# One matmul on 112 columns for two on 64 and 48 in the state products, and the decay sums F of ten tiles in column quarters

## The chip, the cores and the metric

The kernel runs on one core of one Trainium2 chip. The metric is the device time of one execution in microseconds (us): the median of the executions shown, where one execution is the time of the whole program on that core. A profile is taken of one execution by the hardware profiler; it records every instruction of the five engines with its start and its duration. PE is TensorE's matmuls, PEld its weight loads, DVE is VectorE, ACT is ScalarE, POOL is GpSimd.

## The reference

A gated linear recurrence (batch 4, 8 heads, 768 steps, head dimension 48), and behind it a maxout layer. All is float32.

```python
def _attn_ref(q, k, v, a_re, a_im):
    mag = np.sqrt(a_re * a_re + a_im * a_im)
    scale = np.minimum(mag, 0.999) / (mag + 1e-06)
    a_re_n, a_im_n = (a_re * scale, a_im * scale)
    ...
    for t in range(S):
        ar, ai = (a_re_n[:, :, t, :, None], a_im_n[:, :, t, :, None])
        new_re = ar * S_re - ai * S_im
        new_im = ar * S_im + ai * S_re
        kv = np.einsum('bhd,bhe->bhde', k[:, :, t], v[:, :, t])
        S_re, S_im = (new_re + kv, new_im)
        y[:, :, t] = np.einsum('bhd,bhde->bhe', q[:, :, t], S_re)

def _moe_ref(x, w1, w2, w3, w_out):          # x: 3072 x 384
    h = np.maximum(np.maximum(x @ w1, x @ w2), x @ w3)   # 3072 x 768
    return h @ w_out                          # 3072 x 384
```

## The kernel before, in words

The recurrence is computed in blocks of 128 time steps. There are 24 tiles, one for each batch and block: `x = 2 * g + c`, with g from 0 to 11 and c called x or y in the schedule (`Fx:3` is step F of group 3, c = 0). Six values of g in a row (s = 0 to 5) walk through one pair of batches. A tile holds 8 heads of 48 columns and two chunks of 64 steps; the chunks lie on the two halves of the 128 rows (partitions) of the keys and values.

For each tile the steps on TensorE are, by their names in the schedule:

- `cs` sums the phases along time; `sums` sums the log magnitudes `Ln` within a chunk (64 rows, 64 columns, line 649).
- `F` forms the decay sums of a head for 29 cut positions: the weights are a head's 48 columns of `Ln`, the moving operand is the matrix `cuts` (lines 679 to 695). Two forms stand in the code. The plain one takes each chunk alone: 64 rows, 48 weight columns, 29 moving columns, 16 matmuls a tile. The quartered one takes both chunks at once: 128 rows, weights in pieces of 32 and 16 columns, 58 moving columns (`cuts` has zeros where a row belongs to the other chunk), again 16 matmuls a tile. ScalarE then takes the exponential of the sums (`f0` to `f3`).
- `tpk` and `tpq` transpose the rotated keys and queries, which are 112 columns wide (cosine part in columns 0 to 47, sine part in 64 to 111, zeros between); `A` and `B` are scores, `y` the outputs.
- `dk` (line 802) forms the state products: for each of 8 head and chunk pairs (4 pairs where s = 5) and each of two row halves j, the keys' 64 rows by 112 columns times the values' 64 rows by 48 columns. `h1` and `h3` add the result to the state `g`.

The maxout layer's matmuls are `U..` (tile `up`), `P1` to `P7`, `Px`, `Py` (tile `op`, a seven-product scheme) and, for the first group, `O`. The set-up has `T`, `M` and `pw` matmuls.

The order of all work on every engine is written out by hand: `SCHEDULE` is a list of words `step:group`, and each engine executes its instructions in that order. Three further lists say how a word is executed. `SLOTS` gives each matmul step its PSUM buffer, `OTHER` moves a step to another engine, and `QUARTERS` names the words whose matmuls are issued on column pieces of 32. In the kernel before, `QUARTERS` holds `cs`, `P`, `U` words but no `F` and no `dk`.

So TensorE executes matmuls of five shapes of array tile, by rows and columns: 128 by 128 (`U`, `P`, `O` in the plain form), 128 by 64 (`cs`), 128 by 32 (`A`, `B`, `y` and all quartered words), 64 by 64 (`sums`, `F`, `dk`) and 64 by 128 (`tpk`, `tpq`). Each float32 matmul call appears in the trace as two weight loads and two matmuls; a transpose appears as one of each.

The plain F loops are these lines:

```python
for ch in range(2) if not quarter else ():
    r = slice(ch * L64, (ch + 1) * L64)
    mm(out=ps[o:o + D, ch, n * NF:(n + 1) * NF], lhsT=T["Ln", g][r, h * D:(h + 1) * D],
       rhs=cuts[r, ch], start=True, stop=True)
for lo, hi in ((0, 32), (32, D)) if quarter else ():
    mm(out=T["Fp", x][o + lo:o + hi, :, n * NF:(n + 1) * NF],
       lhsT=T["Ln", g][:, h * D + lo:h * D + hi], rhs=cuts, start=True, stop=True)
```

Of the kernel before, what the change touches and what calls it, by code (L numbers as in the profile page):

```python
# [138 lines left out]
QUARTERS = set("""  # L139
csx:0 csx:1 csx:3 csx:4 Py:2 Px:2 csy:5 csx:5 csx:6 csy:6 csx:8 csx:9 csy:9 csx:10 P1:8 P5:8 P7:8 csy:10 P6:8 Px:8  # L140
Py:8 U12:9 P6:9 Py:9 P2:9 csx:11 csy:11 P4:9 U11:10 U01:10 Py:10 Px:10 U02:10 U12:10 P1:10 U11:11 P2:10 U12:11 P3:10
U01:11 U02:11 Py:11 P1:11 Px:11 P2:11 P5:11 P7:11 P6:11 P3:11 P4:11
""".split())

ROOMS = {0: "w1", 3: "w2", 6: "wo", 11: "w1", 1: "w2", 9: "H", 10: "S", 2: "H", 4: "S", 5: "H", 7: "S", 8: "H"}
# [4 lines left out]
def kernel(  # L150
# [16 lines left out]
    L64 = 64  # L167
    DD = L64 + D
# [28 lines left out]
    T = {}  # L197
# [29 lines left out]
    def banks(nm, n=None):  # L227

        ps = psum.tile([P, 2, 512], FP, tag="ps" + next(slots), name=nm)
        T["ps"] = ps  # L230
        return ps if n is None else ps.rearrange("p a n -> p (a n)")[:, 0:n]
# [149 lines left out]
    def heads(view):  # L381

        dims = [list(d) for d in view.ap]
        return bass.AP(view.tensor, view.offset, dims[:-1] + [[P - D, 2], [1, D]])
# [114 lines left out]
    def both(t, h):  # L499

        return t[:, h]
# [291 lines left out]
    def state(x, name):  # L793

        s = x // C % NS
        G = T["G", x] = gs[x % 4]

        def four(t):

            return heads(t).rearrange("p i j d -> p j i d")  # L800

        if name == "dk":
            ps = T["dk", x] = banks("dk")
            for n in range(H if s < NS - 1 else 4):
                ch, i = divmod(n, 4)
                for j in range(2):
                    r = slice(j * L64, (j + 1) * L64)
                    for lo, hi in ((0, L64), (L64, DD)):
                        mm(out=ps[lo:hi, j, n * D:(n + 1) * D], lhsT=both(T["Uk", x], n)[r, lo:hi],
                           rhs=T["v", x][r, ch, i, j * D:(j + 1) * D], start=True, stop=True)  # L810
        elif name[0] == "h" and name[1:].isdigit():
            c, i = divmod(int(name[1:]), 2)
            new = four(G[0:DD, 1] if c == 0 else gs[(x + C) % 4][0:DD, 0])
            dk = T["dk", x][0:DD, :, 0:DM].rearrange("p j (c i d) -> p c j i d", c=2, d=D) if i else None
            if c > 0 and s == NS - 1 or s + c + i == 0:
                return True
            if i == 0:
                F = T["F", x][0:DD, :, :, CD:CD + 1].rearrange("p (c i) j n -> p c j i n", c=2)
                dve.tensor_tensor(out=new, in0=four(G[0:DD, c]), in1=F[:, c].to_broadcast([DD, 2, 4, D]), op=OP.mult)
            elif s + c == 0:  # L820
                act.copy(out=new, in_=dk[:, c])
            else:
                dve.tensor_tensor(out=new, in0=new, in1=dk[:, c], op=OP.add)
        else:
            return False
        return True
# [158 lines left out]
    def run(name, g):  # L985
# [13 lines left out]
        elif name[0] in "TtMm" and name[1:].isdigit():  # L999
            product(name[0], int(name[1:]))  # L1000
        elif name[0] == "W":
            i = int(name[2:])
            weight_load(i) if name[1] == "L" else weight_step(i, name[1])
        elif name[0] in "Uu" and name[1:].isdigit():
            up(g, int(name[1]), int(name[2]), name[0])
        elif name[0] in "Uu" and name[1:3].isdigit():
            up_one(2 * g + "xy".index(name[3]), int(name[1]), int(name[2]), name[0])
        elif name in SEVEN or name in ("ox", "oy") and g > 0:
            seven(g, name)
        elif name[0] == "J":  # L1010
            join(name[1])
        elif name[-1] in "01" and gates(g, [int(name[-1])], name[:-1]):
            pass
        elif gates(g, list(range(C)), name):
            pass
        else:
            c = "xy".index(name[-1])
            x, name = g * C + c, name[:-1]
            if name in ("Lr", "Li"):
                load_a(g, c, *(("ar", a_re) if name == "Lr" else ("ai", a_im)))  # L1020
            elif name in ("Lk", "Lq"):
                load_kq(g, c, *(("k", k) if name == "Lk" else ("q", q)))
            elif name == "Lv":
                load_v(g, c)
            else:
                assert angles(g, c, name) or turns(g, c, name) or factors(x, name) or scores(x, name) \
                    or state(x, name) or outputs(x, name) or project(x, name), name
# [45 lines left out]
```

## Time and profile before

| | |
|---|---|
| time, median of 2 runs | 543.97 us (543.03 to 544.91) |
| profiled execution, its own time | 543.5 us |
| its span, first to last instruction | 541.8 us |
| mean granted TensorE clock | 0.99 |
| PE busy | 514.8 us (95%), 11146 matmuls |
| PEld busy | 433.8 us (80%) |
| DVE, ACT, POOL busy | 482.4, 362.0, 66.6 us |

The 1.7 us between span and time lie around the program. Almost all lines of the program run through one helper, so that the profile names line 210 for them; the groups are told apart by the tiles that an instruction writes and reads, written out<-in (`dk<-vb,uk`: the state products from values and keys), and by shape (`64*48 64x48`: 64 rows and 48 columns of weights; moving operand of 64 rows and 48 columns). A matmul's recorded duration is its latency; several of them are in flight at once, so the pace is read from starts, or from how long a known number of them takes.

### The profile page before, as it was taken

The page shows a single profiled execution, that of the slowest core. Times are in us where ns is not written, and L with a number is a line of the kernel's source. Part 1 is how long each engine was busy: PE and PEld are TensorE (multiplying, and loading weights), DVE is VectorE, ACT ScalarE, POOL GpSimd, SP SyncE. Part 2 cuts the span into 40 slices and gives each one's busy share as a digit, 9 for nine tenths or more (in the row PEclk, how much of TensorE's full clock was granted, in tenths as well). Part 3 has the DMA queues.
Part 4 walks back from the last instruction along what each step waited for, and adds up shares of the span by engine and source line. Part 5 has one row for each costly group of instructions (what it writes and reads, how often), then busy time and mean ns, then how long its engine had stood idle before and what let it go on. Part 6 is the DMA issues. An engine that isn't in the chain of part 4 may idle for free.

```text
span 541.8 us, 24758 instructions
## 1 busy us (share of the span) xinstructions
PE 514.8 (95%) x11146; PEld 433.8 (80%) x11146; DVE 482.4 (89%) x756; ACT 362.0 (67%) x634; POOL 66.6 (12%) x111
## 2 busy tenths in 40 slices
PE   3499899999999999999899999999999989999996
PEld 1366878788988989888788988888889877977865
DVE  5999999999999899999899989899999879998343
ACT  6999988786777876678697695685763865451100
POOL 8416300200300300100200020020200120000000
PEclk9969999999999999999999999999999999999999
DMA  8999775343154242727024344034153252000001
GB/s 211 287 257 206 174 135 99 65 83 76 32 106 78 57 76 48 137 40 149 4 54 78 69 79 99 4 69 82 26 114 59 37 94 53 19 18 5 4 2 59
DMA packets 140841, 45.27 MB, mean 84 GB/s; under 512 B 130368, under 2 KB 138560, under 8 KB 140736
## 3 DMA queue, kind: packets, MB, share of 16 engines
q1 hardware_dynamic: 136272, 37.76, 32.9%
q0 software_dynamic: 4464, 5.94, 6.4%
q8 instruction: 87, 1.43, 1.1%
q14 instruction: 18, 0.15, 0.1%
HBM read 33.02 MB, written 4.72 MB: 70 GB/s over the span
## 4 chain that ended last, share of the span: by engine, by line
PE 88%; ACT 5%; DVE 2%; issue 2%; POOL 2%; DMA 1%; DVEq 0%; POOLq 0%; ACTq 0%
PE up L210 34%; PE op L210 24%; PE y L210 7%; PE A L210 6%; PE tp L210 4%; PE dk L210 4%; PE sums L210 3%; PE cs L210 2%; PE wm L210 2%; PE F L210 2%; PE B L210 1%; DMA ar<-nf 1%; ACT L210 1%; ACT xhx L210 1%; ACT L L210 1%
## 5 line engine op out<-in xcount | busy, mean ns | idle before, releaser
L210 PE MATMUL up<-xhx,w 128*128 128x256 f32 (+1 forms) x1278 | 179.0, 381 | 1.6 <-issue 1.5
L210 PEld LDWEIGHTS up<-xhx,w 128*128 128x128 f32 (+1 forms) x1278 | 140.3, 149 | 31.0 <-issue 2.9
L210 ACT ACT_TABLE_LOAD x51 | 65.4, 1283 | 1.6 <-PEq L1057 0.8
L210 POOL DMA_DIRECT2D ar<-nf x40 | 32.8, 1246 | 165.0 <-DVE ar L210 131.1
L210 PE MATMUL op<-wo,xhx 128*32 128x192 f32 (+3 forms) x418 | 50.0, 366 | 0.0
L210 ACT COPY atm<-B 32x128 f32<-32x128 f32 x96 | 24.5, 255 | 33.5 <-DVE atm L210 18.2
L210 DVE TENSOR_TENSOR Q<-Q,f 112x512 f32<-112x512 f32 (+1 forms) x48 | 45.0, 951 | 1.0 <-ACT Q L210 1.0
L210 ACT ACTIVATE f<-F 48x232 f32<-48x232 f32 x96 | 34.3, 358 | 15.1 <-PE F L210 9.7
L210 PE MATMUL y<-QG,g 112*32 112x64 f32 x1408 | 38.5, 219 | 1.8 <-issue 1.8
L210 PE MATMUL y<-atm,vb 128*32 128x64 f32 x1152 | 39.2, 220 | 0.9 <-ACT uk L210 0.9
L210 PEld LDWEIGHTS op<-wo,xhx 128*32 128x32 f32 (+1 forms) x418 | 34.4, 139 | 5.6 <-issue 2.4
L210 PEld LDWEIGHTS y<-atm,vb 128*32 128x32 f32 x1152 | 34.1, 109 | 4.8 <-issue 3.7
L210 PEld LDWEIGHTS y<-QG,g 112*32 112x32 f32 x1408 | 35.3, 109 | 2.0 <-issue 1.9
L210 PE MATMUL A<-Q,K 112*32 112x80 f32 x1536 | 32.8, 238 | 0.9 <-ACT t L210 0.9
L210 DVE COPY_PREDICATED atm<-masko,A 128x256 f32<-128x256 uint8 x72 | 31.6, 439 | 1.4
L210 PE MATMUL op<-wo,strassen 128*128 128x192 f32 (+1 forms) x272 | 32.6, 327 | 0.0
L210 PEld LDWEIGHTS A<-Q,K 112*32 112x32 f32 x1536 | 28.9, 112 | 4.6 <-issue 2.0
L210 PE MATMUL op<-w,strassen 128*32 128x192 f32 (+1 forms) x296 | 32.5, 328 | 0.0
L210 PEld LDWEIGHTS op<-wo,strassen 128*128 128x128 f32 (+1 forms) x272 | 28.4, 152 | 2.3
L210 DVE TENSOR_TENSOR ot<-ot,op 128x384 f32<-128x384 f32 (+1 forms) x56 | 25.6, 464 | 4.2 <-PE op L210 3.5
L210 PEld LDWEIGHTS op<-w,strassen 128*32 128x32 f32 (+1 forms) x296 | 28.0, 147 | 1.6 <-issue 0.3
L210 DVE TENSOR_TENSOR xhx<-xhx,up 128x768 f32<-128x768 f32 x22 | 20.9, 949 | 9.0 <-PE up L210 8.9
(152 smaller groups left out, 1048.9 us busy)
## 6 DMA issues: line engine op xcount, KB each, us to landing
ai<-in_a_im_dram SPq DMA_DIRECT2D x24, 192.0 KB, 3.9
ar<-in_a_re_dram SPq DMA_DIRECT2D x24, 192.0 KB, 3.3
q<-in_q_dram SPq DMA_DIRECT2D x96, 48.0 KB, 2.7
k<-in_k_dram SPq DMA_DIRECT2D x96, 48.0 KB, 2.7
vb<-in_v_dram SPq DMA_DIRECT2D x96, 48.0 KB, 3.1
out_dram<-ot SPq DMA_DIRECT2D x23, 192.0 KB, 3.1
Ln<-e POOLq DMA_DIRECT2D x8, 384.0 KB, 5.7
w<-in_moe_w_dram SPq DMA_DIRECT2D x3, 767.2 KB, 7.3
```

The lines of the kernel that those rows point to most:

```text
L210: ins = f(*a, **kw)
```

## The change

All 24 `dk` words and ten `F` words (`Fx:2` to `Fx:11`) are added to `QUARTERS`. For `F` this chooses the quartered form that is in the code. For `dk` the loop over column pieces now asks the list too: a `dk` word in it issues one matmul on all 112 columns in place of one on columns 0 to 63 and one on columns 64 to 111. The schedule's order, the PSUM buffers and the engines stay.

```diff
 QUARTERS = set("""
 ...
-U01:11 U02:11 Py:11 P1:11 Px:11 P2:11 P5:11 P7:11 P6:11 P3:11 P4:11
+U01:11 U02:11 Py:11 P1:11 Px:11 P2:11 P5:11 P7:11 P6:11 P3:11 P4:11 dkx:0 dky:0 dkx:1 dky:1 dkx:2 dky:2 dkx:3 dky:3
+dkx:4 dky:4 dkx:5 dky:5 dkx:6 dky:6 dkx:7 dky:7 dkx:8 dky:8 dkx:9 dky:9 dkx:10 dky:10 dkx:11 dky:11 Fx:2 Fx:3 Fx:4
+Fx:5 Fx:6 Fx:7 Fx:8 Fx:9 Fx:10 Fx:11
 """.split())
...
                 for j in range(2):
                     r = slice(j * L64, (j + 1) * L64)
-                    for lo, hi in ((0, L64), (L64, DD)):
+                    for lo, hi in ((0, DD),) if T["word"] in QUARTERS else ((0, L64), (L64, DD)):
                         mm(out=ps[lo:hi, j, n * D:(n + 1) * D], lhsT=both(T["Uk", x], n)[r, lo:hi],
                            rhs=T["v", x][r, ch, i, j * D:(j + 1) * D], start=True, stop=True)
```

## The prediction

> **What bounds the kernel now.** I read the page's totals and its chain first, then TensorE's share by stretch and its waits, and only then the instructions that change.
>
> ```profile
> span 541.8 us, 24758 instructions
> PE 514.8 (95%) x11146; PEld 433.8 (80%) x11146; DVE 482.4 (89%) x756; ACT 362.0 (67%) x634; POOL 66.6 (12%) x111
> ...
> PE 88%; ACT 5%; DVE 2%; issue 2%; POOL 2%; DMA 1%; DVEq 0%; POOLq 0%; ACTq 0%
> ```
>
> ```profile
> core 0: us, PE busy (x) PEld busy (x) DVE busy (x) ACT busy (x) POOL busy (x), PEclk, DMA share, GB/s
> 0.00:72.00 72.00, 52.87 (x902) 38.09 (x902) 63.75 (x104) 65.40 (x118) 31.75 (x69) 0.93 0.93 224
> 72.00:500.00 428.00, 424.47 (x9445) 367.72 (x9444) 402.83 (x626) 294.75 (x511) 34.88 (x42) 1.00 0.35 66
> ```
>
> ```profile
> PE y L210 <- issue: 1.8, 1, 1.8
> PE up L210 <- issue: 1.5, 1, 1.5
> ```
>
> The first fence gives TensorE 88% of the chain that ended last. The second, busy time by stretch, shows where: before 72 us it works 53 of 72 us, from 72 to 500 us all but 3.5 of 428 us, at the full granted clock. The third, TensorE's waits after 72 us, names those 3.5 us: two pauses in which it waited for nothing that the profile shows. So behind 72 us no other engine delays TensorE, and what its stream gains or loses there moves the end one for one. Only two of the 24 `dk` steps lie ahead, and only the second, at 57 us, has cover, for the chain runs over VectorE there:
>
> ```profile
> 38.86 1.12 PE dk L210 x53
> ...
> 57.65 0.95 DVE ai L210
> 58.60 0.87 DVE w L210
> ```
>
> **What the two steps cost today.** The trace does not give an instruction's pace by its duration, since several are in flight. I take it from starts, comparing a single with a double burst that were entered alike, so that entry and exit cancel.
>
> ```profile
> 102.31 1.09 PE L210 MATMUL dk<-vb,uk 64*64 64x48 f32 x64
> 103.33 0.27 PE L210 MATMUL tp<-ident,uq 64*112 64x64 f32 x2
> ...
> 291.92 2.02 PE L210 MATMUL dk<-vb,uk 64*64 64x48 f32 x128
> 293.87 0.43 PE L210 MATMUL op<-w,strassen 128*128 128x192 f32 x1
> ...
> 141.03 0.56 PE L210 MATMUL F<-cuts,Ln 64*48 64x29 f32 x32
> 141.51 0.26 PE L210 MATMUL y<-atm,vb 128*32 128x64 f32 x4
> ...
> 270.67 0.92 PE L210 MATMUL F<-cuts,Ln 64*48 64x29 f32 x64
> 271.52 0.48 PE L210 MATMUL up<-xhx,w 128*128 128x256 f32 x1
> ...
> 169.35 0.46 PE L210 MATMUL B<-QB,KB 112*32 112x32 f32 x32
> 169.62 0.39 PE L210 MATMUL cs<-w,upto 128*32 128x192 f32 x4
> ```
>
> `dk`: 128 matmuls take 1.95 us (291.92 to 293.87), 64 take 1.02 us. The 64 more cost 0.93 us. They go in turn to four array tiles (two row halves by columns 0-63 and 64-111), 16 to each, so a tile with 64 weight columns takes 58 ns a matmul. `F`: 32 more cost 0.85 - 0.48 = 0.37 us, 8 on each of four tiles: 46 ns. `B`: 32 in 0.27 us, 8 on each of four column tiles: 34 ns.
>
> What sets these paces? Not the moving operand: F moves 29 columns and takes 46 ns, B moves 32 and takes 34. By weight columns they stand in order: 32 gives 34 ns, 48 gives 46, 64 gives 58, which is 12 ns for each 16 columns. The weight loads say the same:
>
> ```profile
> L210 PEld LDWEIGHTS up<-xhx,w 128*128 128x128 f32 x630 | 117.8, 190 | 19.3 <-issue 2.5 <-ACT Ek L210 0.3 <-ACT Q L210 0.3
> L210 PEld LDWEIGHTS y<-atm,vb 128*32 128x32 f32 x1152 | 34.1, 109 | 4.8 <-issue 3.7 <-ACT atm L210 0.3 <-ACT CS L210 0.2
> L210 PEld LDWEIGHTS dk<-vb,uk 64*64 64x64 f32 x704 | 22.5, 135 | 5.5 <-issue 2.2 <-DVE nf L210 1.5 <-DVE atm L210 0.6
> L210 PEld LDWEIGHTS dk<-vb,uk 64*48 64x48 f32 x704 | 20.3, 119 | 0.0
> L210 PEld LDWEIGHTS tp<-ident,uq 64*112 64x112 f32 x384 | 12.9, 133 | 3.7 <-issue 1.8 <-PE tp L210 0.9 <-ACT En L210 0.3
> L210 PEld LDWEIGHTS wt<-ident,w 128*128 128x128 f32 x18 | 2.1, 141 | 0.7 <-issue 0.4
> ```
>
> Mean durations are 109, 119, 135 and 190 ns for 32, 48, 64 and 128 columns, whether on 64 or on 128 rows: (190 - 109) / 96 = 0.84 ns a column. Transposes load faster: 128 columns in 141 ns (`wt`), 112 in 133 (`tp`). So `dk` and `F` are bound by their weight loads, four of which run side by side.
>
> **The change part by part.**
>
> *dk's loads.* Per pair and row half one load of 112 columns takes the place of two side by side, of 64 and 48. The trace's 1408 loads on four tiles, 352 each, become 704 on two row halves, again 352 each, one after the other on each half. Matmul count halves, but the number of loads that must follow one another does not, and each is longer. No load of 112 columns that is not a transpose stands in the trace. Its pace is bounded from below by `tp` (112 columns on two row halves) and from above by a plain 128-column matmul:
>
> ```profile
> 479.59 1.93 PE tp L210 x64
> ...
> 325.56 1.04 PE tp L210 x32
> ...
> 74.81 1.53 PE up L210 x12
> ```
>
> In the chain, 32 more transposes cost 0.89 us, 16 on each half: 56 ns. That also shows that the two halves load side by side. Twelve `up` matmuls with 128 columns of weights and 128 moving columns take 1.53 us: 127 ns each. Between 56 and 127 ns I extend the line of the untransposed loads: 58 + 48 x 0.84 = 98 ns. The nearer row in kind is `dk`'s own load, not the transpose. So 352 x (98 - 58) = +14.1 us; the ends are 352 x (56 - 58) = -0.7 and 352 x (127 - 58) = +24.3 us.
>
> [...]
>
> *Changes of array shape.* TensorE pauses when two neighbouring steps use different shapes:
>
> ```profile
> 347.50 0.56 PE L210 MATMUL F<-cuts,Ln 64*48 64x29 f32 x32
> 347.88 0.37 PE L210 MATMUL sums<-Ln,mid 64*64 64x192 f32 x3
> ```
>
> F's 32 matmuls occupy 0.38 us when `sums` (also 64 by 64) follows, but 0.48 us when `y` (128 by 32) follows, above. The change of shape costs 0.10 us; I take 0.11, because a step with longer matmuls than F's, such as `sums`, has more to empty. The order puts `dk` beside `sums` and `F`: all three are 64 by 64 today. With `dk` at 64 by 128 and ten F at 128 by 32, counting neighbours in the schedule's order of TensorE words, 30 changes are new (nearly all `dk` or `F` beside `sums` or another F) and 8 go (`y` before or after `Fx`, `Fx` before `A`, `tp` beside `dk`): 153 become 175. 22 x 0.11 = +2.4 us. Bounds: 1.5, were the entry partly hidden, to 3.5, at 0.16 us each as behind `sums`, whose 192 moving columns last longer.
>
> *F.* Sixteen calls stay sixteen, on four column tiles. Loads shrink to 32 or 16 columns, and 58 moving columns become the limit. The nearest row moves 64:
>
> ```profile
> 505.93 1.72 PE y L210 x112
> ```
>
> 112 in 1.72 us less one shape change (0.11) is 1.61 / 28 = 57 ns on a tile; 6 columns less at 0.84 ns gives 52. Against 46 ns that is 8 x 6 = 0.05 us a step, +0.5 us for ten; bounds 0 (F's pace kept) and 1.0 (y's pace 57). ScalarE's exponentials read the same number of columns.
>
> *What is cheaper or free.* 1408 fewer TensorE instructions cost nothing elsewhere; none of `dk`'s readers changes. They get its result 0.6 us later: VectorE and ScalarE add it to `g`, and VectorE has 25 us of idle time between 72 and 500 us (402.83 of 428 busy) while TensorE, the later one, is what it waits for. No step gets a new dependency.
>
> *Sum.* 14.1 + 2.4 + 0.5 = 17.0 us; less 0.6 for the second burst, which lies where TensorE has idle time, is +16.4 us. Against the profiled execution's own time of 543.5 us (span 541.8 and 1.7 around it) this gives 559.9, 560 us. The median of the runs shown, 543.97, is 0.5 us above it, so the ratio is 1.03.
>
> **The rivals.**
>
> *The transposes' pace holds for dk (on the other side).* If a 64-row load of 112 columns costs what `tp`'s does, the burst stays as long as now: -0.7 + 2.9 = +2.2, 546 us. It decides if the pace comes out below some 80 ns. For it: same rows, same columns, same tiles. Against it: `wt` and `up` load the same 128 columns in 141 and 190 ns, so the transpose is a cheaper kind.
>
> *The number of instructions sets the price.*
>
> ```profile
> PE up L210 34%; PE op L210 24%; PE y L210 7%; PE A L210 6%; PE tp L210 4%; PE dk L210 4%; PE sums L210 3%; PE cs L210 2%; PE wm L210 2%; PE F L210 2%; PE B L210 1%; DMA ar<-nf 1%; ACT L210 1%; ACT xhx L210 1%; ACT L L210 1%
> ```
>
> `dk` is 4% of the chain, 21 us; half the matmuls would save 10.5 us, and with +2.9 the time is 536 us. Against it: the cost per matmul is 8 ns in B (0.27 / 32), 11 in F and 14.5 in `dk`, so it is no constant. [...]
>
> *The two row halves load in turn.* Then 704 x 98 = 69 us stand against 20.4 (352 x 58): +48.6 + 2.9, 595 us. Against it: `tp`'s two halves at 56 ns.
>
> **How the numbers follow.** The load-bound forecast has 0.80; its own range is 554 to 564 (pace 95 to 103 ns, the bounds of the other terms, and the two pauses of 3.3 us gone or not). The transposes' pace has 0.11, the instruction count 0.05, loads in turn 0.03; 0.01 is left for a gain that no row shows. The whole range, 552 to 567, reaches down to a pace of 85 ns with the pauses gone (352 x 27 = 9.5, + 2.9 - 0.6 - 3.3) and up to 117 ns (352 x 59 = 20.8, + 2.9 - 0.6); it leaves out the rivals, 0.2 in all. A measurement of this kernel tells about 2% from no change, 10.9 us: slower is 0.80 + 0.03 = 0.83, within 2% 0.11 + 0.05 = 0.16 (546 and 536 are +0.4% and -1.4%), faster 0.01.
>
> **What would show it.** Right: loads `dk<-vb,uk` 64x112 with a mean near 175 ns (135 + 48 x 0.84); a full `dk` burst of 32 matmuls from 1.6 to 1.75 us where it took 1.0; `sums` or `F` beginning 0.1 us later after `dk`; TensorE's chain share up, its waits after 72 us unchanged; F steps at 0.41 to 0.55 us. Wrong: a mean of 130 ns and a burst near 1.0 us (first rival), 0.5 us (second), or over 3 us (third); or new waits of other engines that take up the 16 us.

## The result, and the profile after

The changed kernel takes 573.03 us (median of 571.16 and 574.91) against 543.97 us before: ratio 1.0534, 95% interval 1.0367 to 1.0702. The forecast was slower, 560 us, with a range up to 567. So the sign was right and the size was not: the loss is 29 us where 16 were forecast. The profiled execution took 571.16 us, its span is 569.5 us, 27.7 us more than before.

Page of the changed kernel: totals, and the chain that ended last.

```profile
span 569.5 us, 23350 instructions
PE 537.4 (94%) x10442; PEld 453.2 (80%) x10442; DVE 483.8 (85%) x756; ACT 362.7 (64%) x634; POOL 66.4 (12%) x111
...
PE 89%; ACT 5%; issue 3%; DVE 1%; POOL 1%; DVEq 0%; POOLq 0%
PE up L212 34%; PE op L212 23%; PE y L212 7%; PE dk L212 6%; PE A L212 5%; PE tp L212 4%; PE sums L212 3%; PE cs L212 2%; PE F L212 2%; PE B L212 1%; ACT L L212 1%; ACT xhx L212 1%; PE wm L212 1%; POOL cuts L212 0%; ACT f L212 0%
```

TensorE still makes the chain, `dk` has gone from 4% to 6% of it, and "issue", the time in which TensorE waited for nothing that the profile shows, from 2% to 3%. First the instructions that changed: weight loads by shape, and bursts in order of time (start, duration from first start to last end; the next step's start ends the burst).

```profile
L212 PEld LDWEIGHTS dk<-vb,uk 64*112 64x112 f32 x704 | 36.8, 175 | 7.4 <-issue 4.3 <-DVE nf L212 1.5 <-ACT e L212 0.5
```

```profile
188.60 1.77 PE L212 MATMUL dk<-vb,uk 64*112 64x48 f32 x32
190.31 0.43 PE L212 MATMUL op<-wo,strassen 128*128 128x192 f32 x1
...
363.69 0.59 PE L212 MATMUL F<-cuts,Ln 128*32 128x58 f32 x32
364.21 0.39 PE L212 MATMUL sums<-Ln,mid 64*64 64x192 f32 x4
```

The load of 112 columns has a mean of 175 ns, as forecast (135 + 48 x 0.84), and a full `dk` burst takes 1.71 us to the next shape, in the forecast window of 1.6 to 1.75. F takes 0.52 us to the next shape, in its window too. Now the waits of TensorE behind 72 us, which I had expected to stay as they were:

```profile
PE F L212 <- issue: 4.0, 2, 2.6
PE y L212 <- issue: 2.5, 3, 1.1
PE A L212 <- issue: 1.6, 2, 1.0
PE B L212 <- issue: 0.7, 1, 0.7
```

Two pauses of 3.3 us in all have become eight of 8.8 us. They lie in B, A, F and y. `dk`'s new form leaves the instructions of these steps as they were; of the four only F has a new form of its own, and the pauses stay without it (see `dk` alone, below). Last the granted clock (PEclk, first the changed kernel, then the kernel before):

```profile
54.00:58.00 4.00, 1.96 (x34) 0.98 1.01 261
58.00:65.00 7.00, 7.00 (x114) 0.52 0.10 23
65.00:457.00 392.00, 384.16 (x7297) 1.00 0.37 71
457.00:460.00 3.00, 3.00 (x12) 0.53 0.12 21
460.00:569.00 109.00, 103.95 (x2434) 1.00 0.10 27
```

```profile
54.00:65.00 11.00, 9.75 (x257) 1.00 0.62 148
65.00:541.00 476.00, 468.72 (x10341) 1.00 0.33 64
```

The granted clock was 0.52 in the 7 us near 60 us and 0.53 in the 3 us behind the longest pause; in the kernel before it was 1.00 at both places. The clock records of the trace have 0.50 for 6.83 us from 57.84 us on and for 3.41 us from 457.20 us on: half clock. My estimate, if the work goes as the clock does, is 7 x 0.48 + 3 x 0.47 = 4.8 us lost. The 36 `up` matmuls from 457.00 us on fit it: they take 9.65 us, where 36 others, from 331.77 us on, take 7.97, and half of 3.41 us is 1.71.

### The profile page after: what moved, and what is told of

The parts are those of the page before. It is cut to its first block, busy times and chain, and to the rows that moved or that the text cites. A ratio compares the mean times of both kernels' runs of the same rounds, so it can differ in the third digit from the quotient of the medians.

```text
span 569.5 us, 23350 instructions
## 1 busy us (share of the span) xinstructions
PE 537.4 (94%) x10442; PEld 453.2 (80%) x10442; DVE 483.8 (85%) x756; ACT 362.7 (64%) x634; POOL 66.4 (12%) x111
## 4 chain that ended last, share of the span: by engine, by line
PE 89%; ACT 5%; issue 3%; DVE 1%; POOL 1%; DVEq 0%; POOLq 0%
PE up L212 34%; PE op L212 23%; PE y L212 7%; PE dk L212 6%; PE A L212 5%; PE tp L212 4%; PE sums L212 3%; PE cs L212 2%; PE F L212 2%; PE B L212 1%; ACT L L212 1%; ACT xhx L212 1%; PE wm L212 1%; POOL cuts L212 0%; ACT f L212 0%
## 5 line engine op out<-in xcount | busy, mean ns | idle before, releaser
L212 PEld LDWEIGHTS up<-xhx,w 128*128 128x128 f32 (+1 forms) x1278 | 141.9, 150 | 29.7 <-issue 1.2
L212 ACT ACTIVATE f<-F 48x232 f32<-48x232 f32 x96 | 34.4, 359 | 20.4 <-PE F L212 14.6
L212 PEld LDWEIGHTS dk<-vb,uk 64*112 64x112 f32 x704 | 36.8, 175 | 7.4 <-issue 4.3
L212 PE MATMUL y<-atm,vb 128*32 128x64 f32 x1152 | 40.1, 223 | 2.0 <-issue 1.1
L212 PE MATMUL dk<-vb,uk 64*112 64x48 f32 x704 | 39.6, 261 | 2.0 <-DVE nf L212 1.1
```

What stands on the lines that cost most here:

```text
L212: ins = f(*a, **kw)
```

## The experiments

There are two theories. **P (position):** the extra pauses are instruction fetch, by which I mean that TensorE waits for a packet of the DMA queue that the trace marks "instruction", and where they fall is fixed by where an instruction stands in TensorE's stream. **L (load):** they belong to `dk`'s longer products, to what waits behind them, or to the chance of one execution.

P comes from counting. One DMA queue of the trace, q8, marked "instruction", carries 82 packets of 16,384 bytes in the changed kernel (87 before), about one for each 256 of the 21,029 records of TensorE (22,437 before: loads, matmuls and the instructions that only wait); I take it for TensorE's. By estimate that is 16,384 / 256 = 64 bytes an instruction. Busy time of TensorE from the start up to four of the pauses, with the number of its matmuls and loads:

```profile
0.00:269.80 269.80, 250.18 (x4540) 209.58 (x4540) 244.76 (x382) 207.65 (x358) 46.55 (x87) 0.97 0.54 116
0.00:281.60 281.60, 260.94 (x4794) 218.84 (x4794) 254.41 (x398) 214.81 (x372) 49.84 (x91) 0.97 0.52 111
...
0.00:443.20 443.20, 419.72 (x7720) 358.86 (x7721) 399.10 (x621) 321.52 (x553) 61.44 (x105) 0.98 0.44 93
0.00:453.30 453.30, 429.28 (x7974) 367.54 (x7975) 406.79 (x637) 327.98 (x564) 63.15 (x107) 0.98 0.44 92
```

From the first pause to the second, and from the third to the fourth, 254 + 254 = 508 loads and matmuls pass, and each time four waiting instructions of TensorE's own lie between: 512, twice 256. Counted so over the whole trace, all nine longer pauses of the changed kernel (one lies ahead of 72 us) and both of the kernel before begin at the same place, 193 above a multiple of 256, and all end 1.3 to 1.5 us after a 16 KB packet of that queue has landed. The same holds in the traces of all twelve kernels of this document: of 85 pauses over 0.3 us behind 72 us, 84 begin at such a place and end 1.2 to 1.6 us after a packet has landed, and none of the 1027 such places is passed earlier than 1.2 us after its packet (packet n belongs to place 256 n + 193). The other pause, 0.33 us, waits for VectorE. The kernel before and the changed one have 167 of the 1027 places, and the earliest is passed 1.40 and 1.25 us after its packet has landed. The longest one in order of time:

```profile
452.84 0.47 PE L212 MATMUL F<-cuts,Ln 128*32 128x58 f32 x20
455.87 0.33 PE L212 MATMUL F<-cuts,Ln 128*32 128x58 f32 x10 [2.56 <-issue]
```

So in these traces every 256th instruction is a place that TensorE passed only 1.2 us or more after its packet had landed; I call it a fetch place. That the pauses come where a stretch of small matmuls is there too early is the reading of P, and the runs below try it. `dk` on one matmul takes 64 instructions from each full burst, and so moves the places through all later steps.

**Shifting the kernel before by 64 places.** Idle matmuls behind the first transposes, in a gap of set-up in which TensorE waits.

```diff
                     pe.transpose(out=ps[:, o:o + P], in_=ws[0][:, d, ...], identity=ident)
+            for i in range(16 if f == 0 else 0):
+                o = 32 * (i % 4)
+                mm(out=T["ps"][o:o + 32, 1, 480:488], lhsT=ident[:, o:o + 32], rhs=ident[:, 0:8], start=True, stop=True)
```

> The kernel before, with 16 small extra matmul calls (64 TensorE instructions, 32 columns of the identity times 8 columns, into PSUM columns that nobody reads) behind the first transposes of set-up, in a gap of 3 us in which TensorE waits for VectorE. Nothing else differs; every later TensorE instruction stands 64 places further back in the stream. Theory P (position): in the traces TensorE's unexplained pauses all begin where the count of its instructions is 193 over a multiple of 256, and end 1.2 to 1.4 us after an instruction fetch of 16 KB (256 instructions of 64 bytes) has landed; a dense stretch pauses where such a place falls into it. Then a shift by 64 places, which costs no work, costs 5 to 15 us in some 10 to 16 pauses of 0.3 to 1.3 us: 549 to 558 us. Rival L (load): the pauses belong to the changed kernel's longer products, or are chance of the execution; then this kernel takes 543 to 545 us.

Measured 563.8 us, ratio 1.0357 (1.0301 to 1.0414): 64 idle instructions in a gap of set-up make the kernel 19.5 us slower, 6 us above P's window. P is right in kind and was too low in size. The waits of this kernel behind 72 us:

```profile
PE F L210 <- issue: 5.9, 3, 2.6
PE y L210 <- issue: 3.4, 3, 2.6
PE B L210 <- issue: 3.3, 3, 1.1
PE A L210 <- issue: 2.5, 2, 1.7
PE op L210 <- issue: 1.8, 2, 1.1
PE dk L210 <- issue: 0.8, 1, 0.8
PE sums L210 <- issue: 0.7, 1, 0.7
PE up L210 <- issue: 0.6, 1, 0.6
PE tp L210 <- issue: 0.6, 1, 0.6
```

They sum to 19.6 us, 16.3 more than the kernel before has, with no `dk` or F changed. The profiled execution was the slowest of its kernel, with a span 24.0 us longer than before's, so the pauses are two thirds of its loss; some 3 us more are half clock, in two stretches of 3.4 us behind the pauses at 278.6 and 452.6 us.

**Shifting it by 256 places, a whole packet** (the same edit with `range(64 if f == 0 else 0)`).

> As the kernel with 64 extra instructions, but 256 of them (64 calls), still inside the same gap: every later instruction stands a whole block of 256 places further back. Theory P: the places of the pauses relative to the work are those of the kernel before, so the time is that of the kernel before, 543 to 546 us, although four times as many instructions were added. Rival L: also 543 to 546 us. A rival by which extra instructions as such cost time (their fetch): over 549 us, and four times the loss of the 64.

Measured 543.29 us, ratio 0.9978 (0.9957 to 1.0000). Four times as many instructions cost nothing that shows:

```profile
PE y L210 <- issue: 2.6, 2, 1.9
PE up L210 <- issue: 1.6, 1, 1.6
```

The pauses are again in `y` and `up`, as in the kernel before. L fell with the shift by 64, for it said 543 to 545 us there; here the idea falls that instructions as such cost time.

**Shifts by 32 and by 240** (`range(8 ...)`, `range(60 ...)`).

> The kernel before with 8 idle matmul calls (32 TensorE instructions) in the gap of set-up. Theory P: the loss depends on where the fetch places fall, not on how many instructions are added. Replaying the stream of the kernel before with each place 256 i + 193 held until about 3.4 us after the stream has passed 304 instructions ahead of it gives pauses of 12 us for a shift by 64 (measured 19.5 us slower), 5.4 us for 32 and 1 us for 240 (which is 16 back). So this kernel takes 548 to 554 us. Rival: no position effect below half a block, or the same loss for every shift: 544 or 563 us.

> The kernel before with 60 idle calls (240 instructions, a shift of 16 places back). Theory P, by the same replay: 1 us of new pauses beside those that it has, some of which may go: 542 to 547 us. Rival by which 240 extra instructions cost like 64: 563 us.

The replay's 304 and 3.4 us are estimates from the traces: in those of the kernel before and of the changed one no packet starts while its place is more than 296 and 294 instructions away, and TensorE never passes a place sooner than 3.5 and 3.1 us after it stood 304 instructions ahead of it.

Measured 549.0 us, ratio 1.0090 (1.0066 to 1.0115), and 546.19 us, ratio 1.0040 (1.0023 to 1.0058). Both lie in P's windows. In order of shift, 0, 32, 64, 240 and 256 give 544, 549, 564, 546 and 543 us: the loss depends on the place, not on the count.

**The change's two parts, each alone.**

```diff
 # only dk: the list without the ten F words
-dkx:10 dky:10 dkx:11 dky:11 Fx:2 Fx:3 Fx:4
-Fx:5 Fx:6 Fx:7 Fx:8 Fx:9 Fx:10 Fx:11
+dkx:10 dky:10 dkx:11 dky:11
 # only F: the list without the 24 dk words
```

> The change without its F part: dk on 112 columns, F in the plain form throughout. Theory P with the sum of the prediction: loads +14.1 us, 21 more changes of array shape +2.3 us, and the pauses of the changed kernel (the instruction stream has the same length step by step, as F has 16 calls in both forms): 566 to 572 us. Rival: the 11 us beyond the forecast come from F's quartered form (its steps longer than thought, or its wait on both chunks): then this kernel takes 558 to 561 us.

> The change without its dk part: ten F steps in column quarters, dk as before. Theory P: the instruction stream keeps its length at every step, so no pause is added; F +0.5 us, 2 more changes of array shape +0.2 us: 543.5 to 545.5 us. Rival by which F brings the missing 11 us: 553 to 556 us.

Measured 573.61 us, ratio 1.0520 (1.0467 to 1.0573), and 543.71 us, ratio 0.9989 (0.9963 to 1.0014). The whole loss is `dk`'s; it lies 1.6 us above the window. F in quarters, which keeps 16 calls and so every place, makes no difference that shows. The pauses of `dk` alone lie in the steps of the changed kernel's (one of 0.3 us in `up` is added), though F has its old form:

```profile
PE F L212 <- issue: 4.0, 2, 2.5
PE y L212 <- issue: 3.3, 3, 1.9
PE A L212 <- issue: 2.1, 2, 1.2
PE B L212 <- issue: 1.0, 1, 1.0
PE up L212 <- issue: 0.3, 1, 0.3
```

**The changed kernel with the lost instructions put back.** If P holds, doing more must make it faster.

```diff
         T["word"] = "%s:%d" % (name, g)
+        if name in ("dkx", "dky"):
+            T["owed"] = T.get("owed", 0) + (2 * H if g % NS < NS - 1 else H)
...
         T["ps"] = ps
+        for i in range(T.pop("owed", 0) if nm in ("y", "A", "B") else 0):
+            o = 32 * (i % 4)
+            mm(out=ps[o:o + 32, 1, 480:481], lhsT=ident[:, o:o + 32], rhs=ident[:, 0:1], start=True, stop=True)
```

(The fillers load 32 columns and move one, where the expectation says one weight column.)

> The changed kernel, with the 64 TensorE instructions that each dk step lost put back (32 for a dk of four pairs) as 16 (8) idle matmul calls on one weight column and one moving column, ahead of the next y, A or B step, which has their array shape. So from that step on every instruction stands where it stood in the kernel before, counted modulo 256. Leaves nothing out. The fillers cost at most B's pace, 8.4 ns for a load and its matmul: 704 x 8.4 = 6 us. Theory P (the 11 us beyond the forecast are pauses of instruction fetch, fixed by place): the pauses behind 72 us go back to the 3 to 5 us of the kernel before, and the time is 544 + 14.1 + 2.4 + 0.5 + 2 to 6 = 563 to 567 us, faster than the changed kernel though it does more. Rival L (the 11 us belong to dk itself or to what its length delays): 573 + 2 to 6 = 575 to 579 us.

Measured 569.3 us, ratio 1.0451 (1.0425 to 1.0476): faster than the changed kernel's 573.0, and 6 to 10 us below L's window. All four executions lie below both of the changed kernel's, but that kernel was executed only twice, and its interval (1.0367 to 1.0702) takes this ratio in. The time is 2 us above P's window; the clock was 0.76 from 58 to 65 us here, which is 1.7 us. Its waits, and one group of fillers:

```profile
PE y L212 <- issue: 1.5, 2, 1.0
PE up L212 <- issue: 0.7, 1, 0.7
PE B L212 <- issue: 0.6, 1, 0.6
```

```profile
451.82 0.43 PE L212 MATMUL y<-ident 128*32 128x1 f32 x32
452.09 0.31 PE L212 MATMUL y<-atm,vb 128*32 128x64 f32 x8
```

2.8 us of pauses are left (before: 3.3). 32 fillers take 0.27 us, so by estimate 704 take 5.9 us; without them 569.3 would be 563.4 us.

**The changed kernel shifted by 96 places** (the first edit with `range(24 ...)`, in the changed kernel).

> The changed kernel with 24 idle calls (96 instructions) in the same gap. Its removed instructions change the places anew at each dk step, so no single shift restores them; the replay gives 3.4 us of pauses for a shift of 96 where it gives 5.6 for none. Theory P: 567 to 573 us, with the pauses at other steps than in the changed kernel. Rival L: 573 us with the pauses at the same steps.

Measured 563.08 us, ratio 1.0355 (1.0332 to 1.0378), 4 us below P's window, so more was gained than expected: 96 idle instructions make the changed kernel 10 us faster. Pauses and clock of this kernel:

```profile
PE F L212 <- issue: 1.4, 1, 1.4
PE A L212 <- issue: 1.3, 1, 1.3
PE y L212 <- issue: 1.1, 2, 0.9
PE up L212 <- issue: 0.4, 1, 0.4
```

```profile
54.00:58.00 4.00, 2.76 (x78) 1.00 1.18 262
58.00:65.00 7.00, 7.00 (x134) 0.76 0.18 45
65.00:562.00 497.00, 488.76 (x9721) 1.00 0.32 62
```

There are 4.2 us of pauses, and half clock only near 60 us, 7 x 0.24 = 1.7 us. As P expects, the pauses are not those of the changed kernel: F's two, at 283 and 456 us there, are gone, and one stands in an F that had none, at 198.5 us; only the one in `A` is in a step that paused before, 0.9 us earlier in it.

**dk with twice the moving columns**, to see what its pace hangs on.

```diff
-                        mm(out=ps[lo:hi, j, n * D:(n + 1) * D], lhsT=both(T["Uk", x], n)[r, lo:hi],
-                           rhs=T["v", x][r, ch, i, j * D:(j + 1) * D], start=True, stop=True)
+                        st, m = 2 * n * D + j * D, D if 2 * n + j == 2 * H - 1 else 2 * D
+                        mm(out=ps[lo:hi, j, n * D:n * D + m], lhsT=both(T["Uk", x], n)[r, lo:hi],
+                           rhs=T["v", x].rearrange("p c i d -> p (c i d)")[r, st:st + m], start=True, stop=True)
```

> The changed kernel with each dk matmul moving 96 columns in place of 48 (the next pair's columns too, whose products are then written over by their own matmul); weights, counts and places are unchanged. Theory W: dk on 112 columns is bound by its weight load, 98 ns on each row half; 96 columns move in some 80 ns and hide under it, so a full dk burst keeps its 1.70 us to the next step and the time stays within 2 us of the changed kernel's, 571 to 575 us. Rival M: the moving columns or the matmul itself set the pace; then each of the 352 matmuls of a half takes 40 ns more, a burst 2.3 us, and the time is 14 us longer, 587 us.

Measured 571.23 us, ratio 1.0502 (1.0473 to 1.0532). The same burst as above takes 1.74 us where it took 1.71:

```profile
187.66 1.81 PE L212 MATMUL dk<-vb,uk 64*112 64x96 f32 x32
189.40 0.43 PE L212 MATMUL op<-wo,strassen 128*128 128x192 f32 x1
```

Doubling what the matmuls move costs 0.03 us a burst, so the load sets the pace of this burst and the moving operand does not. The 80 and 40 ns of the expectation fit 96 and 48 columns at the 0.84 ns that the prediction measured on loads; as the pace of moving columns they are estimates, and no run shows them.

**dk in four column pieces**, the opposite of the change: more and smaller matmuls.

```diff
-                    for lo, hi in ((0, L64), (L64, DD)):
+                    for lo, hi in ((0, 32), (32, L64), (L64, 96), (96, DD)):
```

> The kernel before with dk in four column pieces of 32, 32, 32 and 16 (eight array tiles of 64 rows by 32 columns), F as before. Theory W: each tile loads 32 columns 16 times a burst, B's pace of 34 ns by the load or some 43 ns by 48 moving columns, so a burst without pauses takes 16 x 43 = 0.69 us and 0.14 to the next shape, 0.83 us where the kernel before has 0.95 to 1.07 us: 352 x (43 - 58) = -5.3 us in all. Theory P: a full burst has 256 TensorE instructions in 0.7 us, a whole fetch block, so there are pauses in or behind most bursts, and the places of all later steps move by 128: some 15 to 30 us more, so 555 to 575 us. Rival without position: -5.3 us and 21 changes of shape at 0.11 us, 541 us.

Measured 584.31 us, ratio 1.0752 (1.0692 to 1.0811), outside the window. The pauses in `dk` came as expected,

```profile
PE dk L210 <- issue: 10.8, 7, 2.1
```

but the pace did not. A half burst of 64 matmuls takes 0.59 us from its first start to its last in the records, 9 ns each, where 43 ns (an estimate, 48/64 of `y`'s 57) on eight tiles would be 5.4. Its first 32 matmuls come near the expected pace, 0.19 us or 6 ns each; the other 32 take 0.39 us, 12 ns each. Five full bursts of 128, four with one of the places in them and one without, all last 1.16 us, so these are not the pauses at the places. What holds the later matmuls back I did not try.

The time is 9 us above the window. All waits of this kernel for "issue" behind 72 us sum to 20.4 us, 17.1 more than before's, of a span that is 40.1 us longer. The slower pace and five more stretches of half clock, 3.4 us each, are part of the rest.

## Why the prediction was right or wrong

**What bounds the kernel:** right. TensorE makes 89% of the chain, and the lag that `dk` brings is not made up later: behind 73 us it shrinks by more than 0.15 us only at the two pauses that the kernel before has and the changed one has not.

**The load term, +14.1 us:** right. The forecast was 175 ns a load in the trace and a pace of 98; the load has 175, a full burst takes 1.71 us and a double one (389.20 to 392.48 us) 3.28, so 16 loads more on each half cost 1.57 us, 98 ns each. The kernel with wide moving operands shows that the load is the bound of this burst: 1.74 us with 96 moving columns, 1.71 with 48. All three rivals of the prediction fall: the burst is neither 1.0 us (transposes' pace), nor 0.5 us (count), nor over 3 us (loads in turn). The load of 112 columns takes 56 ns more than that of 48 (means of 175 and 119 in the traces), 0.88 ns a column.

**Shape changes and F, +2.4 and +0.5 us:** together with the loads they hold to within 1 us. The count of shape changes, 153 and 175, is that of the traces' matmuls in order of start. Both traces have the same 9738 matmuls other than `dk` in the same order, so the lag of the changed kernel can be read from their starts, step by step. From 72 us to the end it grows from 2.7 to 27.6 us:

| where the lag grows | us |
|---|---|
| the 22 `dk` steps, with the changes of shape into and out of them | 15.5 |
| F | 0.9 |
| fetch places of the changed kernel | 10.7 |
| fetch places of the kernel before (pauses that went) | -3.5 |
| half clock behind the longest pause | 1.5 |
| all else | -0.2 |

The sum has 17.0 us less 1.3 for the loads of the two `dk` steps ahead of 72 us, which is 15.7, where the first, second and last row show 16.2. The same reading gives 15.8 at `dk` and 0.8 at F for the kernel shifted by 96 places. The refilled kernel, whose pauses sum to 2.8 us, agrees: less 5.9 us for its fillers and 1.7 for half clock it is 17 us slower than before, where the sum said 16.4. F alone shows nothing, within its interval of -0.4% to +0.1%.

**The second burst's cover, -0.6 us:** wrong. I let it vanish under VectorE's work, and by 72 us the changed kernel is 2.8 us behind instead (the F step that starts at 69.11 us before starts at 71.93). A pause of 0.91 us at a fetch place, up to 57.78 us, falls into that burst, and the rows of 58 to 65 us show half clock behind it (0.52 over the 7 us), which I had not considered at all; in the kernel with wide moving operands, where the clock stayed at 1.00, it is about 1 us. Four of the five kernels with `dk` on 112 columns have half clock there, for 3.4 or 6.8 us, and none of the six with `dk` in its old form has it. Why is not shown.

**"1408 fewer TensorE instructions cost nothing elsewhere":** this is the step that failed, and with it the forecast that TensorE's waits after 72 us stay unchanged. I priced what the removed instructions had cost, and not that every later instruction changes its place, counted modulo 256. The prediction saw the two pauses of "issue", 3.3 us, and took them as something that stays or goes; it asked neither what they were nor why the kernel had only two. The runs show that the kernel before stands at a favourable place: a shift by 32 or 64 costs it 5 or 19.5 us. The change moved off that place. By the table the fetch places cost 10.7 - 3.5 = 7.2 us more than before. (The lists of waits show 5.5, for they count a pause from the end of the last matmul in flight, some 0.2 us behind its start.) With 1.5 us of half clock behind the longest pause and 2.0 of the 2.7 us lost by 72 us (the sum has 0.7 there) this is 10.7 us, nearly all of the 11.3 us by which the longer span, +27.7, misses the sum, +16.4.

## What to carry to other kernels

In this kernel, whose stream of small matmuls ran with two pauses behind 72 us, part of the tuning was where the instructions stand: 64 idle instructions alone moved it by 3.6%, 256 by nothing that shows (ratio 0.9978). So judge a change of the instruction count with the pauses told apart, or try it at several shifts. Half as many matmuls were not cheaper in `dk`, where the weight load sets the pace: two loads side by side on 64 and 48 columns cost 58 ns, one on 112 costs 98. Before extending a matmul over more columns, compare paces by weight columns and by moving columns, and see which one they follow.

## What the runs showed of the hardware

The pauses at 193 above a multiple of 256 I had not expected. In the kernel shifted by 64 places they take up to 2.6 us each, and its pauses sum to 16.3 us more than those of the kernel before. In all twelve traces no two of the 16,384-byte packets land closer together than 3.2 us (3.22 in the kernel before and in the changed one), while F, with 64 instructions in 0.52 us, would by estimate pass 256 in some 2.1 us. By these two numbers a stretch at F's pace, were it long enough, would come to a fetch place before its packet. Why the place is 193, and why one packet lands later than another, is not shown.

Half clock, a granted clock of 0.50 in the records, lasted 3.4 us at a time, once 6.8 us, between 72 us and the last matmul. Nine such stretches stand there in the twelve traces, and all of them begin during a pause of 1.6 us or more or within 1.5 us behind one; the changed kernel's, from 457.20 us on, stands 1.3 us behind the pause of 2.56 us. It does not follow each time: twelve other pauses of 1.6 to 2.65 us have none behind them, among them the 1.75 us of the kernel before, whose clock is 1.00 from 35.6 to 540.8 us, and the 2.45 us of the kernel with wide moving operands, whose clock is 1.00 from 65 us on. What decides between the two is not shown.
